# Two-layer decode attention on one core: V becomes the moving operand of the value product, in column tiles

## The chip, the cores and the metric

One core of a Trainium2 chip runs the whole program. The metric is device time in microseconds (us) of one execution, as the median of several runs. A core has five engines with an instruction queue each: TensorE (PE in the profile; PEld is its weight load), VectorE (DVE), ScalarE (ACT), GpSimd (POOL) and SyncE (SP), which here issues every transfer. Sixteen DMA engines move data between HBM and the on-chip memory SBUF. TensorE writes into PSUM, eight banks of 128 partitions by 512 fp32.

## The reference, cut to what matters

Eight sequences decode one token each through attention, a small dense block, and the same two again with the same weights and caches. The caches are 8 x 8 x 8192 x 128 in bf16, K and V, 134 MB each, and both layers need all of both.

```python
q = (x @ wq) -> 8 sequences, 32 heads, 128
k = repeat(k_cache, 4 times over heads)       # 8 cache heads, 4 query heads share one
scores = q . k * 128 ** -0.5                   # 8192 keys per sequence and cache head
p = softmax(scores)
o = p . v
x = x + o @ wo                                 # on layernorm(x)
x = x + silu(layernorm(x) @ w1) @ w2
# both steps once more
```

## The kernel before, in words

A task is (layer, sequence, cache head): 2 x 8 x 8 = 128 of them. The 8192 keys of a task are cut into four granules of 2048. A granule of K or V is one transfer of 512 KB into one of 27 slots of a large SBUF buffer (`ARENA`), 4 KB on each partition. Positions are half granules, so a task has `GPT` = 8 positions, and the main loop runs over positions `p`. The order of all work is the order of emission in that loop; each engine executes its own instructions in that order, and every wait follows from which buffers an instruction reads and writes.

The last 20 of the 32 K granules of a sequence (cache heads 3 to 7) stay in their slots from layer 0 to layer 1; these are the "kept" keys. So 352 K transfers and 512 V transfers are made, not 512 and 512. `make_tasks` orders the tasks so that, for each sequence in turn, come its five kept tasks of layer 0, then other tasks of layer 0 and 1 that load both K and V, then its five tasks of layer 1 whose keys are already there. While the kept keys of a sequence are resident, 20 of the 27 slots are taken and 7 are left for streaming; when they are used up, more slots are free. `plan_loads` gives every transfer a slot, ordered by the position that needs it; SP issues them in that order (`issue`), and waits before each until the slot's last reader, a matmul, is done.

What a task does, by position within it (`ph` = p mod 8):

- DVE transposes each loaded K granule in place, 32 x 32 words at a time (`emit_t`, L444), two positions ahead of its use.
- `emit_q` (L463, L466): four matmuls place the task's four query vectors in QSp, and DVE writes them, masked, into the stationary tile QB.
- `emit_s` (L481): at each odd position 16 matmuls score one granule. Scores are made in four column tiles of 32: tile `t` has its own 32 rows of the PSUM bank SCp.
- `softmax_max` at ph 0 of the next task (L491, L493): DVE takes the row maxima and spreads them; `softmax_shift` at ph 2 (L501 to L507): an fp32 matmul of ones sums these over partitions into OTp, and DVE picks each row's shared maximum. The exponentials are made by ACT right behind (L511).
- `softmax_sum` at ph 4 (L518, L521): row sums by DVE, joined over partitions by GpSimd's partition_all_reduce.
- `emit_pt` at ph 5 (L530, L534): TensorE transposes P, DVE copies it to PT.
- `emit_pv` (L554), `LP` = 14 positions behind the scores: 16 matmuls for each granule, each with a 128 x 128 block of V as the stationary operand and 4 probability columns, repeated `PVN` = 12 times to 48, as the moving one. The sum of a whole task stands in one bank OTp.
- `emit_norm` (L568), one position after the last of these: DVE divides by the row sums into the attention output.

When the last task of layer 0 of a sequence is normalized, a chain of small stages follows, a few per position: output projection (L652), layernorm (L576 to L612), both dense products and the query of layer 1 (L634). It has to be done before the sequence's first layer-1 task.

Of the kernel before, what the change touches and what calls it, by code (L numbers as in the profile page):

```python
# [5 lines left out]
HQ = 32  # L6
DH = 128
SM_SCALE = DH ** -0.5
# [22 lines left out]
PVN = 12  # L31
# [97 lines left out]
class Load:  # L129


    __slots__ = ("kind", "b", "g", "k", "need", "free", "slot", "after")

    def __init__(self, kind, b, g, k, need, free):
        self.kind, self.b, self.g, self.k = kind, b, g, k
        self.need, self.free = need, free
        self.slot, self.after = None, None
# [33 lines left out]
def plan_loads(tasks, kept, nslot, ngran):  # L171
# [3 lines left out]
    for i, (layer, b, g) in enumerate(tasks):  # L175
        for k in range(ngran):
            i0 = i * GPT + k * GPG
            if layer == 0 or (g, k) not in kept:
                need = -1 if i0 < PRE else i0 - LT
                last = i if layer or (g, k) not in kept else at[(1, b, g)]  # L180
                loads.append(Load("K", b, g, k, need, last * GPT + (k + 1) * GPG - 1))
# [3 lines left out]
    for d in loads:  # L185
# [3 lines left out]
        free.append((d.free, d.slot))  # L189
    return loads  # L190
# [18 lines left out]
def _build(ctx, nc, A_x, A_k_cache, A_v_cache, A_wq, A_wo, B_w1, B_w2, out):  # L209
# [64 lines left out]
    pick = sb([128, NPART, 128], BF16, "pick")  # L274
# [15 lines left out]
    PT = [sb([128, CPB, NQ * USED], BF16, "PT") for _ in range(NPT)]  # L290
    ones = sb([128, 128], FP32, "ones")
    hm = sb([128, REP], FP32, "hm")
    real = sb([128, 1], FP32, "real")
    far = sb([128, NQ * USED], FP32, "far")
    rowmax = sb([128, 1], FP32, "rowmax")
    spread = sb([128, NQ * USED], FP32, "spread")
    own = sb([128, NQ * USED], FP32, "own")
# [56 lines left out]
    k_slot = {}  # L354
    v_slot = {}

    def issue(d):
# [7 lines left out]
        (k_slot if d.kind == "K" else v_slot)[(d.b, d.g, d.k)] = d.slot  # L365

    with nc.Block() as block:

        @block.sync
        def _(sync_eng):  # L370
# [11 lines left out]
            op(dve, lambda: dve.memset(ones[:, :], 1.0), writes=["ones"])  # L382
            for n in range(NQB):
# [5 lines left out]
                    hm[:, :], lanes.rearrange("p c (r k) -> p r c k", k=NGRAN), AX.XY, ALU.add),  # L389
                reads=["ident"], writes=["hm"],  # L390
            )
            op(dve, lambda: dve.tensor_reduce(real[:, :], hm[:, :], AX.X, ALU.add), reads=["hm"], writes=["real"])
# [3 lines left out]
            for i in range(NPART):  # L396
                op(dve, lambda i=i: dve.tensor_copy(
                    pick[:, i, :].rearrange("p (a r) -> p a r", a=NQ),
                    ident[:, i // 2 * 2 * QUAD:(i // 2 + 1) * 2 * QUAD].rearrange("p (r e) -> p e r", e=2)[:, i % 2]
                    .unsqueeze(1).to_broadcast([128, NQ, QUAD])),  # L400
                   reads=["ident"], writes=["pick"])
            for c in range(NQ):
                op(dve, lambda c=c: dve.tensor_scalar(
                    far[:, c * USED:(c + 1) * USED].rearrange("p (r k) -> p r k", k=NGRAN),
# [365 lines left out]
            for p in range(NG + LP + GPT + 1):  # L770
# [8 lines left out]
                if p % GPG == GPG - 1:  # L779
                    if p < NG:  # L780
                        emit_s(p)
# [77 lines left out]
```

## Time and profile before

| | us |
|---|---|
| median of 3 runs | 1194.06 (1191.72 to 1194.8) |
| the profiled execution | 1198.79 |
| its span, first to last instruction | 1197.1 |
| DMA queue of SP, share of 16 engines' span | 99.1% |
| PE busy, VectorE busy, ScalarE busy, GpSimd busy | 839.0, 736.1, 183.5, 70.8 |
| instructions | 46189 |
| mean granted TensorE clock | 0.663 |

465.05 MB are read from HBM at 388 GB/s over the span. A busy share is an average over stages that differ: the DMA engines are busy nearly throughout, and what they move in 20 us varies between 333 and 410 GB/s. So the rate in each stage is to be read, not the share alone.

### The profile page before, as it was taken

What the parts mean: (1) busy time and instruction counts of PE and PEld (TensorE: products, weight loads), DVE (VectorE), ACT (ScalarE), POOL (GpSimd) and SP (SyncE); (2) the same over time, 40 slices, a digit from 0 to 9 for tenths busy, and PEclk for the clock granted to TensorE, in tenths of its full rate; (3) what the DMA queues carried; (4) which work ended last, traced back from release to release, by engine and by line L of the source; (5) the groups of instructions that cost most, each with busy time, mean ns of one, the idle gap of its engine ahead of it and who ended that gap; (6) DMA issues with size and microseconds to landing.
All of it is one profiled execution on the core that took longest, in us unless ns stands there. A gap on an engine that the chain in (4) does not pass through costs nothing.

```text
span 1197.1 us, 46189 instructions
## 1 busy us (share of the span) xinstructions
PE 839.0 (70%) x20984; PEld 673.4 (56%) x20984; DVE 736.1 (61%) x1830; ACT 183.5 (15%) x266; POOL 70.8 (6%) x172
## 2 busy tenths in 40 slices
PE   1636677767776677767777778777776777677785
PEld 1435566556655566556665566556665656555564
DVE  3736763767456673867457763867376755768464
ACT  0101112111111012111111111111111111111111
POOL 0000000000000000000000000000000000000000
PEclk9955568555765577655866586756775587657765
DMA  9999999999999999999999999999999999999994
GB/s 368 385 396 397 399 355 408 407 394 395 393 408 407 368 389 401 408 404 395 389 408 408 388 397 409 407 402 395 393 407 403 399 393 408 407 392 386 402 408 165
DMA packets 131619, 468.06 MB, mean 391 GB/s; under 512 B 13904, under 2 KB 19808, under 8 KB 130912
## 3 DMA queue, kind: packets, MB, share of 16 engines
q1 hardware_dynamic: 131424, 465.12, 99.1%
q8 instruction: 164, 2.69, 0.9%
q14 instruction: 31, 0.25, 0.1%
HBM read 465.05 MB, written 0.01 MB: 388 GB/s over the span
## 4 chain that ended last, share of the span: by engine, by line
DMA 40%; PE 31%; DVE 15%; issue 9%; SPq 3%; ACT 2%; POOL 0%; POOLq 0%; ACTq 0%; DVEq 0%
DMA arena<-in_A_v_cache_dram 37%; PE OTp L554 14%; PE SCp L481 8%; DVE arena L444 7%; SPq L339 3%; DMA arena<-in_A_k_cache_dram 3%; PE MISC L634 3%; PE OTp L501 2%; PE TPp L530 2%; ACT P L511 2%; DVE rowmax L491 1%; DVE PT L534 1%; PE MISC L652 1%; DVE tr L607 1%; DVE spread L493 1%
## 5 line engine op out<-in xcount | busy, mean ns | idle before, releaser
L554 PE MATMUL OTp<-PT,arena 128*128 128x48 bf16 x8192 | 381.1, 205 | 227.6 <-DMA arena<-in_A_v_cache_dram 182.1
L444 DVE STREAM_TRANSPOSE arena<-arena 128x1024 int32<-128x1024 int32 x352 | 434.9, 1236 | 115.9 <-DMA arena<-in_A_k_cache_dram 115.2
L554 PEld LDWEIGHTS OTp<-PT,arena 128*128 128x128 bf16 x8192 | 316.9, 110 | 331.5 <-DMA arena<-in_A_v_cache_dram 242.6
L511 ACT ACTIVATE P<-SCp,shift 128x512 bf16<-128x512 f32 x128 | 180.3, 1409 | 930.6 <-DVE shift L507 651.5
L481 PE MATMUL SCp<-arena,QB 128*32 128x128 bf16 x8192 | 287.0, 275 | 37.3 <-issue 29.0
L481 PEld LDWEIGHTS SCp<-arena,QB 128*32 128x32 bf16 x8192 | 161.4, 115 | 84.1 <-issue 48.6
L521 POOL PARTITION_ALL_REDUCE ssa<-ssm x128 | 55.6, 435 | 996.0 <-DVE ssm L518 970.8
L534 DVE COPY PT<-TPp 128x256 bf16<-128x256 bf16 x128 | 37.3, 291 | 103.6 <-PE TPp L530 101.8
L501 PE MATMUL OTp<-spread,ones 128*128 128x64 f32 x256 | 75.4, 389 | 25.9 <-DVE spread L493 22.7
L491 DVE TENSOR_REDUCE rowmax<-SCp 128x1 f32<-128x512 f32 x128 | 84.8, 663 | 11.5 <-PE SCp L481 10.3
L530 PE MATMUL TPp<-ident,P 128*128 128x128 bf16 x512 | 68.8, 278 | 13.7 <-ACT P L511 9.6
L504 DVE SCALAR_TENSOR_TENSOR own<-OTp,real,far 128x64 f32<-128x64 f32 x128 | 32.9, 257 | 71.7 <-PE OTp L501 71.7
L501 PEld LDWEIGHTS OTp<-spread,ones 128*128 128x128 f32 x256 | 54.9, 266 | 35.6 <-DVE spread L493 34.4
L518 DVE TENSOR_SCALAR ssm<-hm,rs 128x4 f32<-128x4 f32 x128 | 26.8, 210 | 73.9 <-ACT P L511 73.9
L530 PEld LDWEIGHTS TPp<-ident,P 128*128 128x128 bf16 x512 | 41.7, 122 | 16.5 <-ACT P L511 12.3
L634 PE MATMUL MISC<-xnT,wq 128*128 128x32 bf16 (+1 forms) x1152 | 37.1, 185 | 19.3 <-DVE xnT L621 13.1
L634 PEld LDWEIGHTS MISC<-xnT,wq 128*128 128x128 bf16 x1152 | 35.8, 105 | 20.4 <-issue 16.3
L652 PE MATMUL MISC<-at,wo 128*128 128x32 bf16 x1024 | 37.7, 185 | 6.1 <-issue 4.4
L652 PEld LDWEIGHTS MISC<-at,wo 128*128 128x128 bf16 x1024 | 33.2, 103 | 6.9 <-issue 4.6
L463 PE MATMUL QSp<-QT,pick 128*128 128x4 bf16 x512 | 32.5, 168 | 5.7 <-DVE QT L717 2.9
L493 DVE TENSOR_SCALAR spread<-ident,rowmax 128x64 f32<-128x64 bf16 x128 | 32.6, 255 | 4.5
L511 ACT ACTIVATION_READ_ACCUMULATOR P<-SCp,shift 128x1 f32 x128 | 33.3, 260 | 0.0
(54 smaller groups left out, 276.3 us busy)
## 6 DMA issues: line engine op xcount, KB each, us to landing
arena<-in_A_v_cache_dram SPq DMA_DIRECT2D x512, 512.0 KB, 10.3
arena<-in_A_k_cache_dram SPq DMA_DIRECT2D x352, 512.0 KB, 14.5
wq<-in_A_wq_dram SPq DMA_DIRECT2D x1, 4096.0 KB, 16.6
wo<-in_A_wo_dram SPq DMA_DIRECT2D x1, 4096.0 KB, 26.3
w<-in_B_w_dram SPq DMA_DIRECT2D x2, 1792.0 KB, 22.8
P<-in_A_x_dram SPq DMA_DIRECT2D x1, 8.0 KB
out_dram<-P SPq DMA_DIRECT2D x1, 8.0 KB
```

The lines of the kernel that those rows point to most:

```text
L444: op(dve, lambda: dve.transpose(words, words), reads=[r_half(slot, 0), r_half(slot, 1)], writes=[r_half(slot, 0), r_half(slot, 1)])
L481: lambda n=n, t=t: pe.matmul(SCp[bank][t * QUAD:(t + 1) * QUAD, k * 128:(k + 1) * 128], QB[qn][:, n, :], keys[:, t, n // 2, n % 2], start= ...
L491: op(dve, lambda: dve.tensor_reduce(rowmax[:, :], SCp[bank][:, :], AX.X, ALU.max), reads=[f"SC{bank}"], writes=["rowmax"])
L493: op(dve, lambda: dve.tensor_scalar(spread[:, :].rearrange("p (c q) -> p c q", q=USED), lanes, rowmax[:, 0:1], -SM_SCALE, op0=ALU.mult, op ...
L501: mm_group([lambda: pe.matmul(every, ones[:, :], spread[:, :], start=True, stop=True)], reads=["ones", "spread"], writes=[f"OT{ob}"])
L511: op(act, lambda: act.activation(P[:, :].rearrange("p (x j k) -> p k x j", x=CPB, k=NGRAN), SCp[bank][:, :].rearrange("p (k x j) -> p k x ...
L521: op(pool, lambda: pool.partition_all_reduce(ssa[st][:, :], ssm[st][:, :], 128, bass.bass_isa.ReduceOp.add), reads=[f"ssm{st}"], writes=[f ...
L530: lambda c=c: pe.transpose(tpv[:, c, :], P[:, c * 128:(c + 1) * 128], ident[:, :])
L534: op(dve, lambda: dve.tensor_copy(PT[pb][:, :, :].rearrange("p x (c q) -> p x c q", q=USED), tpv.rearrange("p x (c q) -> p x c q", q=QUAD) ...
L554: lambda c=c, cc=cc: pe.matmul(otp, chunk(slot, h * GRP + c), pv[:, cc % CPB, cc // CPB % NQ, k, :].unsqueeze(2).to_broadcast([128, REP, P ...
L634: lambda o=o, k=k: pe.matmul(MISC[:, o * n:o * n + w], w_sb[:, k, o * 128:(o + 1) * 128], rhs_of(k).to_broadcast([128, w]) if n == 1 else ...
L652: lambda o=o, h=h: pe.matmul(MISC[:, o * w:(o + 1) * w], wo_sb[:, h, o * 128:(o + 1) * 128], rhs_of(h).to_broadcast([128, w]) if n == 1 el ...
```

## The change

The value product is turned round. V is now the moving operand, 512 columns at a time, and 16 probability columns of one column tile (4 blocks `x` of keys times 4 query rows) are the stationary one. Four matmuls, one for each column tile `t`, do a granule. Each tile has 16 rows of the OTp bank, and of the 512 output columns of a row only the 128 of its own block `x` are wanted. Two ways pick them out. In most tasks ACT copies the whole bank to SBUF as fp32 (`emit_own`, tile E), and four accumulated fp32 matmuls against a selection matrix `sel` (`emit_fold`) join the 64 rows and four blocks into the 128 x 4 result. In the 40 tasks with kept keys in layer 1 (`eased`), four DVE operations add up the own blocks by masks and one fp32 matmul joins them. The result lands in the first columns of OTp as before, and the normalization reads it three positions later than before (`FOLD`).

Two more changes: kept keys of layer 1 are scored two slots at a time, 256 moving columns in each of 16 matmuls, where the distance of the two slots fits (`REACH`), and kept slots come free by pairs; to keep that distance positive the contents of the two slots of a pair may be exchanged, so a transposed slot is looked up by `turn`. And the row maxima are joined over partitions by GpSimd's partition_all_reduce in place of the matmul of ones, with smaller DVE operations around it. The query matmuls now make all heads of a sequence at once (16 matmuls for 8 tasks), and the copy to PT goes from DVE to ACT. The number and size of K and V transfers are unchanged.

```diff
@@ plan_loads
-                loads.append(Load("K", b, g, k, need, last * GPT + (k + 1) * GPG - 1))
+                loads.append(Load("K", b, g, k, need, (last * GPT + (k // PAIR + 1) * PAIR * GPG - 1
+                                  if last != i or PAIR_ALL else last * GPT + (k + 1) * GPG - 1)))
...
+    for pair in keys.values():
+        ks = sorted(d.k for d in pair)
+        for d, k in zip(sorted(pair, key=lambda d: d.slot), ks):
+            d.k = k
@@ emit_q
-                for i in range(NPART):
-                    at = (n * NPART + i) * REP
-                    steps.append(lambda i=i, at=at: pe.matmul(
-                        QSp[:, at:at + REP], pick[:, i, :], q, start=True, stop=True))
+                if ti == span_of[(layer, b)][0]:
+                    emit_queries(layer, b)
...
@@ emit_s
+                two = PAIR_ALL or not has_t(i)
+                if two and k % PAIR != PAIR - 1:
+                    return
+                slots = [k_slot[(b, g, k - n)] for n in range(PAIR - 1, -1, -1)] if two else [t_slot[(b, g, k)]]
+                step = (slots[-1] - slots[0]) * SLOT
...
+                if two and step <= REACH:
+                    runs = [(k - PAIR + 1, k + 1, both)]
...
@@ softmax_max
-                op(dve, lambda: dve.tensor_scalar(
-                    spread[:, :].rearrange("p (c q) -> p c q", q=USED), lanes, rowmax[:, 0:1], -SM_SCALE,
-                    op0=ALU.mult, op1=ALU.mult),
-                   reads=["ident", "rowmax"], writes=["spread"])
+                op(dve, lambda: dve.scalar_tensor_tensor(
+                    top[:, :], hm[:, :], rowmax[:, 0:1], far[:, :], op0=ALU.mult, op1=ALU.add),
+                   reads=["hm", "rowmax", "far"], writes=["top"])
+                op(pool, lambda: pool.partition_all_reduce(tops[:, :], top[:, :], 128, bass.bass_isa.ReduceOp.max),
+                   reads=["top"], writes=["tops"])
@@ softmax_shift
-                mm_group([lambda: pe.matmul(every, ones[:, :], spread[:, :], start=True, stop=True)],
-                         reads=["ones", "spread"], writes=[f"OT{ob}"])
-
                 op(dve, lambda: dve.scalar_tensor_tensor(
-                    own[:, :], every, real[:, 0:1], far[:, :], op0=ALU.mult, op1=ALU.add),
-                   reads=[f"OT{ob}", "real", "far"], writes=["own"])
-                op(dve, lambda: dve.tensor_reduce(shift[:, :], own[:, :], AX.X, ALU.min), reads=["own"], writes=["shift"])
+                    mine[:, :], tops[:, :], -SM_SCALE, hm[:, :], op0=ALU.mult, op1=ALU.mult),
+                   reads=["tops", "hm"], writes=["mine"])
+                op(dve, lambda: dve.tensor_reduce(shift[:, :], mine[:, :], AX.X, ALU.add), reads=["mine"], writes=["shift"])
@@ emit_pt
-                op(dve, lambda: dve.tensor_copy(
-                    PT[pb][:, :, :].rearrange("p x (c q) -> p x c q", q=USED),
-                    tpv.rearrange("p x (c q) -> p x c q", q=QUAD)[:, :, :, 0:USED]),
+                op(act, lambda: act.copy(
+                    PT[pb][:, :, :, :, :].rearrange("p a t x r -> p x t a r"),
+                    tpv.rearrange("p x (t q) -> p x t q", q=QUAD)[:, :, :, 0:USED].rearrange("p x t (a r) -> p x t a r", r=REP)),
                    reads=[f"TP{tb}"], writes=[f"PT{pb}"])
@@ emit_pv
-                        lambda c=c, cc=cc: pe.matmul(
-                            otp, chunk(slot, h * GRP + c), pv[:, cc % CPB, cc // CPB % NQ, k, :].unsqueeze(2).to_broadcast([128, REP, PVN]),
-                            start=(cc == 0), stop=(cc == NCH - 1),
-                        )
+                steps = [
+                    lambda t=t: pe.matmul(
+                        OTp[ob][t * QUAD:t * QUAD + CPB * REP, :], PT[pb][:, k, t].rearrange("p x r -> p (x r)"),
+                        ARENA[:, slot * SLOT + t * KB:slot * SLOT + (t + 1) * KB],
+                        start=(k == 0), stop=(k == NGRAN - 1),
+                    )
+                    for t in range(NQ)
+                ]
+            def emit_own(ti):
+                ob = ti % 2
+                if not eased(ti) and ACT_FOLD:
+                    op(act, lambda: act.copy(E[:, :], OTp[ob][:, :]), reads=[f"OT{ob}"], writes=["E"])
+                    return
+                for x in range(CPB):
...
+                        op(dve, lambda x=x, ot=ot: dve.scalar_tensor_tensor(
+                            E[:, 0:DH], ot, own_x[:, x:x + 1], E[:, 0:DH], op0=ALU.mult, op1=ALU.add),
+                           reads=[f"OT{ob}", "own_x", "E"], writes=["E"])
+            def emit_fold(ti):
...
+                        lambda x=x: pe.matmul(OTp[ob][:, 0:REP], E[:, x * DH:(x + 1) * DH], sel[:, x, :],
+                                              start=(x == 0), stop=(x == CPB - 1))
+                        for x in range(CPB)
...
+                    steps = [lambda: pe.matmul(OTp[ob][:, 0:REP], E[:, 0:DH], hm[:, :], start=True, stop=True)]
@@ main loop
+                copied = p - LP - GPT
+                if copied >= 0 and copied % GPT == 0 and copied // GPT < ntask:
+                    emit_own(copied // GPT)
+                folded = p - LP - GPT - FOLD_AT
+                if folded >= 0 and folded % GPT == 0 and folded // GPT < ntask:
+                    emit_fold(folded // GPT)
...
-                done = p - LP - GPT
+                done = p - LP - GPT - FOLD
```

Constants: `PAIR` = 2, `REACH` = 32767, `FOLD` = 3, `FOLD_AT` = 2, `ACT_FOLD` on, `PAIR_ALL` off. In the startup, `pick`, `ones` and their fills go, and `own_x`, `sel` and two clears of OTp come.

## The prediction

> **What bounds the kernel now.** I read the page's transfer part first, then the rates by stage, then what the transfers wait for.
>
> ```profile
> DMA  9999999999999999999999999999999999999994
> GB/s 368 385 396 397 399 355 408 407 394 395 393 408 407 368 389 401 408 404 395 389 408 408 388 397 409 407 402 395 393 407 403 399 393 408 407 392 386 402 408 165
> q1 hardware_dynamic: 131424, 465.12, 99.1%
> q8 instruction: 164, 2.69, 0.9%
> DMA arena<-in_A_v_cache_dram 37%; PE OTp L554 14%; PE SCp L481 8%; DVE arena L444 7%; SPq L339 3%; DMA arena<-in_A_k_cache_dram 3%; PE MISC L634 3%; PE OTp L501 2%; PE TPp L530 2%; ACT P L511 2%; DVE rowmax L491 1%; DVE PT L534 1%; PE MISC L652 1%; DVE tr L607 1%; DVE spread L493 1%
> ```
>
> The engines are never without packets, the rate is either 407 to 409 GB/s or clearly less, and V transfers head the chain. So the change, which moves the same caches, can only win what lies between a slice's rate and 408. The second line to see is q8: the instructions themselves come through the same 16 engines, in 164 blocks of 16 KB.
>
> Four stages (columns: stage, its length, PE, PEld, DVE, ACT and POOL busy, clock, DMA share, GB/s):
>
> ```profile
> 470.00:515.00 45.00, 32.87 (x761) 25.86 (x761) 30.07 (x64) 7.05 (x10) 2.16 (x5) 0.63 1.03 407
> 390.00:410.00 20.00, 13.93 (x307) 10.81 (x305) 13.52 (x26) 2.81 (x4) 0.83 (x2) 0.50 0.97 349
> 160.00:175.00 15.00, 11.68 (x361) 10.24 (x357) 9.97 (x20) 2.83 (x4) 0.44 (x1) 0.73 0.85 305
> 300.00:320.00 20.00, 16.39 (x470) 14.17 (x471) 11.48 (x34) 2.83 (x4) 0.89 (x2) 0.73 1.01 382
> ```
>
> and what a K transfer takes to land, first in 470:515, then in 390:410:
>
> ```profile
> arena<-in_A_k_cache_dram SPq DMA_DIRECT2D x16, 512.0 KB, 15.6
> ...
> arena<-in_A_k_cache_dram SPq DMA_DIRECT2D x8, 512.0 KB, 7.5
> ```
>
> A transfer of 0.524 MB takes 1.285 us at 408 GB/s. So some 12 are in flight in the first stage and 5 or 6 in the second, where the kept keys leave 7 slots. Every long stretch with 15 us runs at 407; the losses stand where the queue is short. I take the whole span in rows of 20 us and add up (408 - rate) / 408 x 20. From 80 to 1160 us this is 26.8 us: 14.1 us in the ten rows in which a chain's dense stages and query run (160, 300, 440, 560, 580, 700, 820, 840, 960, 1100), 10.9 us in thirteen rows with a short queue, most of it right after the queue gets short (380 and 400 alone 2.9), and 1.8 us scattered. Startup and end are apart.
>
> TensorE in a plain stretch (start, length, ..., [idle before and releaser]):
>
> ```profile
> 271.27 0.82 PE L554 MATMUL OTp<-PT,arena 128*128 128x48 bf16 x16 [0.70 <-DMA arena<-in_A_v_cache_dram]
> 272.16 0.69 PE L501 MATMUL OTp<-spread,ones 128*128 128x64 f32 x2
> 272.78 0.62 PE L481 MATMUL SCp<-arena,QB 128*32 128x128 bf16 x16
> 274.28 0.82 PE L554 MATMUL OTp<-PT,arena 128*128 128x48 bf16 x16 [0.88 <-DMA arena<-in_A_v_cache_dram]
> ```
>
> A granule pair (K and V, 2.57 us) leaves TensorE 0.7 to 1.05 us of waiting for V: it frees slots in time, with little to spare.
>
> **Part by part.**
>
> *Instructions.* Per task there were 64 matmuls for PV, 64 for scores, 4 transposes, 4 query ones and 2 of L501: 138, each with a weight load. Now 88 tasks have 16 + 64 + 4 + 2 and 8 for the fold (L501 shows two instructions for one fp32 matmul): 94. The 40 eased ones have 16 + 32 + 4 + 2 + 2 = 56. That is 88 x 88 + 40 x 164 = 14,300 of 46,189 instructions gone, 31% (28% if no pair of slots fits). At 2.69 MB for all, 0.83 MB less to move: **-2.0 us** (ends -1.8 and -2.3).
>
> *Blocks and the short queue.* A 16 KB block holds up one engine of the sixteen, all others go on, and a K or V transfer has landed only when the last engine has done its share; a long queue hides that until it gets short. That this is the 10.9 us is my inference: it fits where the loss stands, and no row shows it alone. Around such a place 5 of 16 tasks are eased, so instructions there fall by 41%; of 10.9 us: **-4.5 us**. Ends 0 (another cause) and -8.
>
> *PV.* Before: 16 matmuls start to next work in 0.65 us at the half clock. After: 4 tiles of 512 columns. The nearest row is L481, which puts the same 512 columns through each of four tiles in 0.55 us, weight loads included; four serial ones would take 16 x 0.107. I take 0.55, so V's slot is free 0.1 us sooner. Hidden in plain stretches by the wait for V.
>
> *Fold.* Four fp32 matmuls with 128 x 128 weights. The nearest row is L501's pair: 0.69 us in all, of which second weight load starts 0.17 and second matmul 0.27 us after the first. Eight at 0.17 to 0.27: 1.4 to 2.2, plus 0.3 to drain; I take 1.8 at the half clock. It comes after one granule in four: 0.55 + 1.8 + 0.55 = 2.9 against 2.57 us per granule, 0.3 over, and the next granule has 0.9 to make it good. In return L501 (0.62, and 0.2 of waiting for `spread`) goes. Per plain task of 10.3 us TensorE is about even: -0.4 PV, -0.8 L501, -0.1 queries, +1.8. What queues behind the fold are the next score and PV, and behind them the slots; cost taken 0 under five queued transfers (6.4 us), upper end +14 (rival below), lower end -1.
>
> *Eased tasks.* No K to transpose, scores by pairs, one fp32 matmul in place of four: TensorE saves some 2 us of a task of 5.2. The four DVE additions (each nearest to L504's 0.257, 128 columns wide 0.32) are 1.3 us on an engine busy 7 of 20 us there. This follows directly on each chain, where TensorE is at 16.4 of 20 us: the queue refills sooner. Also the page has 74.5 and 48.6 us of weight loads idle for "issue", in stalls up to 2.9 us, of which a third should go. I take a fifth of the 14.1 us: **-3.0 us**. Ends -8, and +5, because `FOLD` starts the chain three positions later with its end fixed: some 22 stages in 18 positions, not 21. Then layernorm's last stage and the first product stand one position apart, not three, and TensorE waits for xnT, about 1 us in each of 7 chains.
>
> *Maxima by GpSimd.* DVE gives up `spread` (0.255) and the long `own` (0.257) for two of 4 columns (L518's row: 0.21), and its 71.7 us of waiting for L501. The reduce is in the trace: L521 0.435 us, and 0.1 from DVE and back. Between `top` and `mine` stands a transposition (1.24 us): hidden. Without that cover, in eased tasks, 0.6 us on a DVE with nothing queued. 0; ends -1, +2.
>
> *Copies on ACT.* PT is 256 elements, E 512; L682's two rows (14 elements 184 ns, 112 elements 265) give 0.83 ns each, L511 2.8 (its store is strided). So PT 0.4 to 0.9 and E 0.6 to 1.6 us, on an engine idle 85%. PT is wanted two positions later, after a score of 0.55 and a V wait of 0.75: covered. 0; ends -1, +2.
>
> *End.* After the last V nothing hides anything: PV -0.2, E +0.6, fold +1.9, two handoffs +0.1: **+2.4 us** (ends +1.6, +3.9). *Start:* 0; SP's long issue of the weights sets it.
>
> Sum: -2.0 - 4.5 - 3.0 + 2.4 = **-7.1 us**. The profiled execution, 1198.79, stands 4.7 over the median of the runs (1194.06) and would come to 1191.7; a median of like runs to **1187.0**.
>
> Two rules of the Trainium skill I weighed. The stages above move 407 GB/s. "DMA: Bandwidth & Descriptors", Specifications, gives HBM about 358 GB/s per core; by it 468.06 MB need 1307 us and nothing could be won. The trace disagrees, and the measurement decides. ACT here loads its tables once (1283 ns). "ScalarE: Activation LUTs", Table sets, says that cheap functions such as copy are in every set, so no reload; no run here shows a copy yet.
>
> **The rivals.**
>
> *Nothing reaches the end* (transfers bound it anyway): the short-queue losses have another cause. -2.0 + 2.4, and up to 3 either way: 1191 to 1197. For it: 99.1%. Against: the rates differ by stage.
>
> *The fold's burst decides* (slower). If its eight passes do not overlap, it takes 8 x (0.27 + 0.2) = 3.8 us. The burst is then 0.55 + 3.8 + 0.55 = 4.9 us, 2.3 over a granule, of which the next makes good some 0.5. The price: in 300:320 the query's four parts of 1.05 us cost 26 / 408 x 20 = 1.3 us, 0.3 for each us. With 47 plain tasks at a short queue (some 480 us of 10.3), each us not made good costs 47 x 0.3 = 14: here 25, and with the -7.1 of the forecast +18, 1212. It decides from half a us not made good, a fold of about 2.5 us. For it: L501's two matmuls take 0.69. Against: nearly half of that is the drain.
>
> *More than that*: all 23 rows at 404: -22 - 2 + 2.4, 1172.
>
> *Others* (column tiles one after the other, 2 us a granule; table reloads of 2 x 1.28 us a task): 1220 and more. Against: L481's 0.55.
>
> **How the numbers follow.** Forecast case 0.47, 1180 to 1191; more 0.10, 1170 to 1180; nothing 0.20, 1191 to 1198; fold 0.16, 1198 to 1220; others 0.07. The likeliest is 1187.0. The range 1177 to 1205 leaves out the lower part of "more", the upper of "fold", and "others". A measurement of this kernel tells 0.3%, 3.6 us, from no change: faster 0.57, same 0.20, slower 0.23.
>
> **What would show it.** Right: q8 near 115 blocks; rows after the queue gets short at 380 or more, deep ones still at 407; the fold's eight matmuls under 2.2 us; the last V's landing to the end about 2.4 us longer (15 before). Wrong: PE or PEld waiting for E or PT, SP waiting longer for the fold's followers, rates under 380 once in each plain task, or a clock that falls and makes PV 0.8 us.

## The result, and the profile after

The changed kernel takes 1201.1 us (median of 7 runs, 1200.1 to 1206.4) against 1194.8 us (7 runs) of the kernel before on the same chip: a ratio of 1.0055, 95% interval 1.0032 to 1.0079, some 6.5 us slower. The forecast was 7 us faster. The profiled execution took 1203.2 us with a span of 1201.2.

From the page of the changed kernel, the rates by slice, the two instruction queues and the chain that ended last:

```profile
GB/s 363 385 396 407 399 376 409 408 403 379 396 409 408 392 357 410 408 399 383 400 409 403 393 391 409 409 392 365 403 408 397 365 396 409 408 404 385 385 409 133
q8 instruction: 109, 1.79, 0.6%
q14 instruction: 35, 0.29, 0.1%
DMA arena<-in_A_v_cache_dram 48%; SPq L356 15%; DMA arena<-in_A_k_cache_dram 10%; PE OTp L608 5%; PE OTp L640 3%; PE MISC L721 3%; DVE arena L466 3%; PE SCp L543 3%; ACT P L570 1%; PE TPp L589 1%; DVE E L632 1%; DVE tr L694 1%; DVE yr L696 1%; DVE rowmax L554 0%; PE MISC L739 0%
```

The deep slices still run at 407 to 410. But there are new holes (357, 365, 365) where the kernel before had 389, 395 and 399. V transfers head the chain with 48% in place of 37%, and SP's issue of loads (L356) has 15% of it in place of 3%: more of the time hangs on transfers and on when they were issued.

From the same page the groups that the change brought (line, engine, operation, count | busy us, mean ns | idle time before, and what ended most of it):

```profile
L608 PE MATMUL OTp<-arena,PT 128*16 128x512 bf16 x2048 | 283.0, 549 | 292.8 <-DMA arena<-in_A_v_cache_dram 289.9
L640 PE MATMUL OTp<-sel,E 128*128 128x4 f32 x704 | 147.9, 333 | 0.9 <-ACT E L624 0.7
L559 POOL PARTITION_ALL_REDUCE tops<-top x128 | 47.5, 371 | 563.1 <-DVE QT L655 241.6
L593 ACT COPY PT<-TPp 128x256 bf16<-128x256 bf16 x128 | 47.6, 372 | 211.7 <-PE TPp L589 211.7
L624 ACT COPY E<-OTp 128x512 f32<-128x512 f32 x88 | 52.1, 592 | 4.1 <-PE OTp L608 4.1
```

PV is 0.55 us a granule; the two ACT copies are 0.37 and 0.59 us. The fold is the one new thing that weighs: 148 us of TensorE in the 88 plain tasks (those that are not eased), 1.68 us each on average and 1.87 us in one piece at the half clock.

Rows of 20 us before (length, busy times of PE, PEld, DVE, ACT and POOL, clock, DMA share, GB/s), a place where the queue gets short and three where a chain runs:

```profile
400.00:420.00 20.00, 13.51 (x296) 10.39 (x292) 13.30 (x32) 1.95 (x3) 1.23 (x3) 0.50 0.99 371
420.00:440.00 20.00, 14.67 (x439) 12.88 (x442) 17.87 (x51) 2.55 (x6) 1.66 (x4) 0.76 1.02 407
680.00:700.00 20.00, 14.11 (x392) 11.85 (x393) 17.49 (x56) 3.00 (x5) 2.45 (x6) 0.75 1.03 407
940.00:960.00 20.00, 15.61 (x408) 13.14 (x404) 16.68 (x49) 2.99 (x5) 2.46 (x6) 0.60 1.02 401
```

The same rows of the changed kernel:

```profile
400.00:420.00 20.00, 12.71 (x223) 7.76 (x224) 14.02 (x38) 4.53 (x8) 2.41 (x6) 0.50 1.01 403
420.00:440.00 20.00, 16.38 (x391) 12.86 (x387) 14.10 (x41) 3.88 (x7) 1.97 (x5) 0.64 0.99 359
680.00:700.00 20.00, 14.77 (x304) 10.81 (x296) 16.52 (x51) 4.28 (x9) 2.68 (x7) 0.59 0.99 376
940.00:960.00 20.00, 13.49 (x292) 9.63 (x292) 15.38 (x44) 3.99 (x8) 2.38 (x6) 0.67 0.97 362
```

Where the queue gets short the change won in three places what the prediction hoped for (371 to 403, and likewise 377 to 394 at 260, 381 to 400 at 660); in three others it lost 8 to 11 GB/s (at 520, 780 and 920). One row later, where the chain starts, it lost more (407 to 359). Summed as in the prediction from 80 to 1160 us, the rows lost 26.8 us before and 30.8 after. The prediction's ten rows with a chain are not where the loss is: they lose 13.1 us in place of 14.1. It stands in rows beside them, where the chains now begin: 280, 420, 680, 800 and 940 lose 9.5 us together in place of 0.9.

What happens there, in TensorE's timeline after, from 416 to 432 (start, length, [idle before and what ended it]):

```profile
416.43 0.61 PE L608 MATMUL OTp<-arena,PT 128*16 128x512 bf16 x4 [1.53 <-DMA arena<-in_A_v_cache_dram]
...
419.05 1.72 PE L721 MATMUL MISC<-xnT,w 128*128 128x32 bf16 x56 [1.47 <-DVE xnT L699]
420.70 0.62 PE L543 MATMUL SCp<-arena,QB 128*32 128x128 bf16 x16
421.11 0.64 PE L608 MATMUL OTp<-arena,PT 128*16 128x512 bf16 x4
421.67 1.87 PE L640 MATMUL OTp<-sel,E 128*128 128x4 f32 x8
...
424.45 1.73 PE L721 MATMUL MISC<-hsT,w 128*128 128x32 bf16 x56
...
431.58 0.61 PE L608 MATMUL OTp<-arena,PT 128*16 128x512 bf16 x4 [3.06 <-DMA arena<-in_A_v_cache_dram]
```

TensorE stands 1.47 us for the LayerNorm's output, and the next granule's matmuls stand behind it in its queue. Then come the first dense product (w1), the fp32 fold and the second product (w2) within 8 us, without a gap to make the delay good. K and V slots come free late, and their loads are issued late. SP's timeline there:

```profile
417.12 0.33 SPq L356 DMA_DIRECT2D arena<-in_A_v_cache_dram  x1
421.41 0.33 SPq L356 DMA_DIRECT2D arena<-in_A_k_cache_dram  x1
421.84 0.38 SPq L356 DMA_DIRECT2D arena<-in_A_v_cache_dram  x1
```

For 4 us no load is issued; the next two go out right after the score and V matmuls that stood behind w1. The loads issued in this stretch take up to 9.5 us to land, and 9.7 us after the V load of 421.84 TensorE comes out of a wait of 3.06 us for V. In the kernel before, w1 waits for nothing at this place, and V is waited for 0.45 to 1.41 us at a time:

```profile
421.99 1.74 PE L634 MATMUL MISC<-xnT,w 128*128 128x32 bf16 x56
...
433.69 0.76 PE L554 MATMUL OTp<-PT,arena 128*128 128x48 bf16 x16 [1.41 <-DMA arena<-in_A_v_cache_dram]
```

The end, from the last copy on (same columns):

```profile
1184.45 0.58 ACT L624 COPY E<-OTp 128x512 f32<-128x512 f32 x1 [4.14 <-PE OTp L608]
1185.09 1.87 PE L640 MATMUL OTp<-sel,E 128*128 128x4 f32 x8 [0.69 <-ACT E L624]
1186.99 0.16 DVE L655 TENSOR_TENSOR QT<-OTp,rcp 128x4 bf16<-128x4 f32 x1 [4.42 <-PE OTp L640]
```

From the last V's landing to the end it is 18.5 us against 15.1: 3.3 more. In the kernel before, the normalization follows the last V matmul directly:

```profile
1182.00 0.82 PE L554 MATMUL OTp<-PT,arena 128*128 128x48 bf16 x16 [0.29 <-DMA arena<-in_A_v_cache_dram]
1182.86 0.16 DVE L568 TENSOR_TENSOR QT<-OTp,rcp 128x4 bf16<-128x4 f32 x1 [3.65 <-PE OTp L554]
```

### The profile page after: what moved, and what is told of

It reads as the page before. It is cut to its first block, busy times and chain, and to the rows that moved or that the text cites. A ratio compares the mean times of both kernels' runs of the same rounds, so it can differ in the third digit from the quotient of the medians.

```text
span 1201.2 us, 32533 instructions
## 1 busy us (share of the span) xinstructions
PE 811.5 (68%) x13960; PEld 505.4 (42%) x13960; DVE 735.7 (61%) x1858; ACT 274.0 (23%) x482; POOL 117.9 (10%) x300
## 4 chain that ended last, share of the span: by engine, by line
DMA 59%; PE 15%; SPq 15%; DVE 7%; issue 3%; ACT 1%; POOL 1%; POOLq 0%; ACTq 0%; DVEq 0%
DMA arena<-in_A_v_cache_dram 48%; SPq L356 15%; DMA arena<-in_A_k_cache_dram 10%; PE OTp L608 5%; PE OTp L640 3%; PE MISC L721 3%; DVE arena L466 3%; PE SCp L543 3%; ACT P L570 1%; PE TPp L589 1%; DVE E L632 1%; DVE tr L694 1%; DVE yr L696 1%; DVE rowmax L554 0%; PE MISC L739 0%
## 5 line engine op out<-in xcount | busy, mean ns | idle before, releaser
L608 PE MATMUL OTp<-arena,PT 128*16 128x512 bf16 x2048 | 283.0, 549 | 292.8 <-DMA arena<-in_A_v_cache_dram 289.9
L543 PE MATMUL SCp<-arena,QB 128*32 128x128 bf16 (+1 forms) x7040 | 275.6, 301 | 3.7 <-DVE mine L563 2.3
L608 PEld LDWEIGHTS OTp<-arena,PT 128*16 128x16 bf16 x2048 | 54.9, 97 | 383.6 <-DMA arena<-in_A_v_cache_dram 375.6
L640 PEld LDWEIGHTS OTp<-sel,E 128*128 128x128 f32 x704 | 140.3, 296 | 37.8 <-issue 25.6
L640 PE MATMUL OTp<-sel,E 128*128 128x4 f32 x704 | 147.9, 333 | 0.9 <-ACT E L624 0.7
L559 POOL PARTITION_ALL_REDUCE tops<-top x128 | 47.5, 371 | 563.1 <-DVE QT L655 241.6
L593 ACT COPY PT<-TPp 128x256 bf16<-128x256 bf16 x128 | 47.6, 372 | 211.7 <-PE TPp L589 211.7
L624 ACT COPY E<-OTp 128x512 f32<-128x512 f32 x88 | 52.1, 592 | 4.1 <-PE OTp L608 4.1
L632 DVE SCALAR_TENSOR_TENSOR E<-OTp,own_x,E 128x128 f32<-128x128 f32 x120 | 42.1, 351 | 4.3
L645 PE MATMUL OTp<-hm,E 128*128 128x4 f32 x80 | 20.5, 327 | 24.1 <-DVE E L632 24.1
```

Of the source, the lines that this page charges most:

```text
L543: lambda n=n, t=t, lo=lo, hi=hi, of=of: pe.matmul(SCp[bank][t * QUAD:(t + 1) * QUAD, lo * 128:hi * 128], QB[qn][:, n, :], of(t, n), start= ...
L608: lambda t=t: pe.matmul(OTp[ob][t * QUAD:t * QUAD + CPB * REP, :], PT[pb][:, k, t].rearrange("p x r -> p (x r)"), ARENA[:, slot * SLOT + t ...
L632: op(dve, lambda x=x, ot=ot: dve.scalar_tensor_tensor(E[:, 0:DH], ot, own_x[:, x:x + 1], E[:, 0:DH], op0=ALU.mult, op1=ALU.add), reads=[f" ...
L640: lambda x=x: pe.matmul(OTp[ob][:, 0:REP], E[:, x * DH:(x + 1) * DH], sel[:, x, :], start=(x == 0), stop=(x == CPB - 1))
```

## The experiments

Two theories to begin with: **late**, that the loss comes from the normalization and the chain that starts behind it coming three positions later (`FOLD` 3), and **burst**, that it comes from the fp32 fold. Ratios are to the kernel before on the same chip; 0.01 is 12 us.

### Three positions later, on the kernel before

Normalization and the bookkeeping behind it, three positions later (the loop runs three positions longer too; cut):

```
-                done = p - LP - GPT
+                done = p - LP - GPT - 3
```

> The kernel before with one thing of the change alone: the normalization, and with it the start of each sequence's chain, 3 positions later. Theory 'chain' (the later start squeezes the chain's stages against its fixed end, TensorE waits for the normalized input and the products come bunched): 3 to 4 us slower than before, 1198, with new losses in the rows 280, 420, 680, 940 and 1100 where the changed kernel has them. Theory 'fold' (the 1.87 us burst of eight fp32 passes holds up scores, PV and so the slots): within 1 us of before.

1.0140 [1.0125, 1.0154], some 17 us where either theory gave 4 at most. In the trace TensorE waits 18.1 us in 23 pieces for the late normalization before L501, which writes the same bank. So that wait is mixed in. The next leaves the normalization alone and moves the bookkeeping only (heads ready for the output projection, start of the chain):

```
                     emit_norm(done // GPT)
+                late = done - 3
+                if late >= 0 and late % GPT == 0 and late // GPT < ntask:
+                    tj = late // GPT
```

> The kernel before, its normalization where it was, and only the bookkeeping behind it (the head given to the output projection, the start of the chain) 3 positions later. In the run with the normalization itself 3 positions later, TensorE's matmul of ones also waited 18.1 us for the normalization, on the bank that the two share. Theory 'chain': most of that run's 16 us stays without this wait, ratio 1.007 to 1.012. Rival 'bank': the shared bank made it, ratio 1.002 to 1.004.

1.0114 [1.0096, 1.0133], some 13.6 us, on a kernel with no fold at all. *Late* holds without the bank. The prediction had put this at 5 us at most.

### Normalization early, and picks in bfloat16

Early, on the changed kernel:

```
-FOLD = 3
-FOLD_AT = 2
+FOLD = 1
+FOLD_AT = 1
```

> The changed kernel with the fold at one position after the copy and the normalization right behind it (2 positions earlier than in the change, 1 later than in the kernel before); the burst itself stays. Theory 'chain': most of the loss goes, 1197 to 1198. Theory 'fold': no change, 1200 to 1202.

1.0082 [1.0062, 1.0103]: not faster. Picks in bfloat16 (in plain tasks `E` and `sel` are rounded to bfloat16; eased tasks keep an fp32 `E32`):

```
-    E = sb([128, CPB * DH], FP32, "E")
+    E = sb([128, CPB * DH], BF16, "E")
+    selb = sb([128, CPB, REP], BF16, "selb")
...
-lambda x=x: pe.matmul(OTp[ob][:, 0:REP], E[:, x * DH:(x + 1) * DH], sel[:, x, :],
+lambda x=x: pe.matmul(OTp[ob][:, 0:REP], E[:, x * DH:(x + 1) * DH], selb[:, x, :],
```

> The changed kernel with the bank copied to SBUF as bf16 and picked by bf16 products in the plain tasks (E is rounded to bf16 there, which the change does not do); the times of all stages stay. The fold should fall from 1.87 to about 0.6 us. Theory 'fold': 4 us or more faster than the changed kernel, under 1197, of which 1.3 us at the end of the program. Theory 'chain': only the 1.3 us at the end, 1200.

0.9995 [0.9982, 1.0009]. Both together:

> Both of the last two edits. If both theories hold a part, this is the fastest of the three, 1190 to 1194, at or under the kernel before; if only 'chain' holds, as the early one less 1.3 us, 1196; if only 'fold' holds, as the bf16 one.

**0.9897 [0.9884, 0.9911]**, 1183.8 us: faster than both kernels, and called the best version below. The fold is 0.27 us here in place of 1.87. So the change holds a gain of some 12 us, and the fp32 fold and the late start together eat 19. They don't add up: the fold alone (early) costs 22, the late start alone (bfloat16) 12. The waits of the early fp32 version show why (waiting, for whom: us, times, longest):

```profile
DVE at L655 <- PE OTp L640: 151.2, 62, 3.9
PE TPp L589 <- ACT P L570: 74.9, 74, 2.4
```

With bfloat16 picks, just as early:

```profile
DVE at L658 <- PE OTp L643: 56.2, 61, 1.8
```

The transposes wait for the exponentials twice as long as in the best version (37.8 us). An early normalization makes VectorE stand 2.4 us at a time, 62 times, behind the fp32 fold, with the next task's softmax in its queue. Three positions later that wait is 13.4 us in all, and the chain pays in its stead. As far as these runs go, `FOLD` chooses only who pays.

With bfloat16 picks and the normalization two positions behind the copy (`FOLD` 2):

> The kernel with bf16 picks and the fold one position after the copy, the normalization 2 positions after the copy (1 in the early one, 3 in the change): a dose in between. Theory 'chain': between 0.9897 and 0.9995, about 0.994. Rival (VectorE's wait for the fold, 56 us in the early one, costs as much as the chain gains): at or under 0.988.

0.9938 [0.9917, 0.9959]: with 0.9897 at one position and 0.9995 at three, 5 to 7 us a position.

### Which part of late: the normalization or the chain

From the best version; the normalization stays early, the bookkeeping comes two positions later (as in `b_chain3`, with `CHAIN` 2):

> The version with bfloat16 picks and the normalization one position after the copy (ratio 0.9897), in which only the bookkeeping behind the normalization (the list of heads ready for the output projection, and the start of the chain between the layers) waits two positions more; the normalization stays. 'Chain' (what the change lost by normalizing late is the late start of the chain, which has a fixed end) expects the whole loss of the version with bfloat16 picks and the normalization three positions behind: a ratio of 0.9975 to 1.001, 9 to 13 us, and the rows at the chains below 400 GB/s. 'Bank' (the late normalization itself holds up the bank of the output, so the matmuls behind it) expects 0.988 to 0.992, nothing lost. Between them each has a share.

1.0007 [0.9990, 1.0024]. The whole loss of late is there; it is the chain's (with the attention heads handed to the output projection, which the edit delays too).

### How a late chain costs

Written out by position from the code, in six of the eight chains all stages from w1 on stand at the same positions however late the chain starts, because its end is fixed (the first and the last chain move as a whole). What a late start does is to put two stages on one position at the chain's beginning. Two ideas: it is the doubling (*squeeze*), or it is the room lost between the LayerNorm's last stage and the first matmul on its output. First, the late chain without its empty stages:

```
-SETTLE = 2
+SETTLE = 0
```

> The version whose chain between the layers starts two positions later (ratio 1.0007) without the chain's four empty stages (two behind each LayerNorm, SETTLE 0 in place of 2): fewer stages in as many positions, so that hardly any position gets two. 'Squeeze' (late start costs because the stages come two to a position against a fixed end) expects most of the 13 us back: a ratio of 0.990 to 0.995. 'Room behind the norm' (the empty stages hide the time to xnT, and matmuls that come without them hold TensorE up for it) expects 1.0007 or worse, up to 1.01, with more waits of TensorE for xnT.

1.0043 [1.0031, 1.0056]: worse than late itself, though nothing is doubled any more. *Squeeze* does not explain the loss: what both have is one position between a LayerNorm and its matmul, here at both LayerNorms. Nor does the late chain double more work than the early one: both put the same two pairs of working stages on one position, and what the late start adds are pairs with an empty stage. TensorE's waits without the empty stages:

```profile
PE MISC L725 <- DVE xnT L703: 12.2, 7, 1.8
PE MISC L725 <- DVE QT L659: 19.0, 7, 2.9
```

The first is w1 behind the first LayerNorm; the second is the query behind the second one (in the trace at 436 us, VectorE makes `QT` directly behind `xnT`). The late chain with its empty stages has 11.3 us of the first and none of the second. Two positions in place of three hurt an early chain too (`SETTLE` 1, with `PAIR` 1):

> The version with ratio 0.9897 with the kept keys scored slot by slot (0.9882 by itself) and one empty stage in place of two behind each LayerNorm of the chain. 'Squeeze' expects a further gain, 0.984 to 0.9875; 'room behind the norm' a loss, 0.989 to 0.993.

1.0026 [1.0013, 1.0040], where `PAIR` 1 alone has 0.9882: 17 us lost. TensorE waits 15 times for the chain's LayerNorm there, 26.8 us, against 4 times and 1.1 us.

Now the room given back without starting earlier: the two dense projections whole, in one stage each, so that the late chain needs two positions fewer:

```
-st = block_stages(xs, ["XT0", "XT1", "XT2"], 1, True)
+st = block_stages(xs, ["XT0", "XT1", "XT2"], 1, False)
```

> The version with bfloat16 picks, early normalization and a late chain (ratio 1.0007), with the chain's two projections of the dense block each emitted whole at one position in place of halves at two. That makes the chain two stages shorter, so that it starts just as late and no stage before the first projection has to go to the position of another: three positions between the LayerNorm's end and the first matmul on its output, as in the version with an early chain; one is left there without this edit. 'Room behind the norm' expects most of the 13 us back, a ratio of 0.989 to 0.994, and TensorE waiting under 2 us in all for that LayerNorm's output (11 us without the edit). 'Late is late' (any later start costs, by vector work that collides with the softmax) expects 0.998 to 1.002.

0.9935 [0.9916, 0.9955]: 8.6 of the 13 us come back, with the start as late as before. Waits with the late chain and its halves (waiting, for whom: us, times, longest):

```profile
PE MISC L725 <- DVE xnT L703: 11.3, 9, 1.6
DVE eh L778 <- ACT eh L773: 9.3, 9, 2.0
```

and with whole projections:

```profile
PE MISC L725 <- DVE hsT L780: 7.4, 8, 1.9
PE MISC L725 <- DVE xnT L703: 2.2, 6, 0.5
DVE eh L778 <- ACT eh L773: 2.0, 1, 2.0
```

Most of the wait for `xnT` goes, and so does most of VectorE's wait for the SiLU's exponential. A new one of 7.4 us for `hsT` comes; that it is the 4.5 us still missing was not tried. From the LayerNorm's last stage to w1 it is three positions in the kernel before, in the best version and here, two at `FOLD` 2 and one in the change, in the six chains named above. One rival stays: an early chain with whole projections was not run, so a part of the 8.6 us could come from the whole projections themselves and not from the room.

The same edit on the change itself, fp32 fold and `FOLD` 3 kept:

> The change itself with the same one edit: the two projections of the dense block whole at one position each. The fp32 picks and their burst of 1.87 us stay, and the normalization stays three positions behind the copy. 'Room behind the norm' expects a ratio of 0.994 to 0.999 in place of 1.0055, that is, the change faster than or level with the kernel before; 'late is late' 1.003 to 1.008.

1.0001 [0.9987, 1.0014] in place of 1.0055: some 6.5 us back by one word. TensorE's wait for the chain's `xnT` is 1.0 us in place of 7.7, and the prediction's ten rows with a chain lose 4.7 us in place of 13.1. The same rival holds here.

### Is it the length of the burst

The best version with the four bfloat16 matmuls of the fold repeated; each repetition begins its sum anew, so that the same four columns come out (the expectation below says otherwise):

```
-                        for x in range(CPB)
+                        for _n in range(TIMES) for x in range(CPB)
```

> The same version (ratio 0.9897) with the four bfloat16 matmuls that fold a plain task's output issued four times over into the same four columns (each start clears the sum... the first, ninth and so on are overwritten, the output's value is not kept): the output's sum is not what the reference wants, and that is all that changes. At the 0.3 to 0.4 us that the four take in bfloat16 this makes a burst of 1.3 to 1.7 us, near the 1.87 us of the fp32 burst of the change, but with the copy of the output in bfloat16 and the normalization early. 'Burst' (the fp32 fold costs by its length on TensorE alone: the score and V matmuls behind it start late, and DVE waits for it) expects most of the 1.85 points between this version and the same with fp32 picks: a ratio of 1.002 to 1.008. 'Other' (the cost of fp32 picks is their weight loads, their clock or the copy in fp32, not the length of the burst) expects 0.989 to 0.995.

0.9905 [0.9892, 0.9918]. But the sixteen matmuls take 0.59 us, not 1.3 to 1.7: some 27 ns for each more. So 0.3 us of burst costs 1 us by the medians, and a long one had still to be run, 15 times over:

> The version with bfloat16 picks and early normalization (ratio 0.9897), the four matmuls of the fold issued 15 times over (each repetition begins its sum anew, so the same four columns come out). Sixteen took 0.59 us in the run with four repetitions, 28 ns for each more, so 60 take about 1.85 us, as long as the fp32 fold of the change. 'Length' (a burst on TensorE costs by its length, in front of score matmuls and of the normalization) expects the ratio of the version with fp32 picks and early normalization, 1.004 to 1.010. 'Something else of fp32' (the copy in fp32, weight loads) expects 0.991 to 0.998.

1.0238 [1.0219, 1.0257], more than either theory gave. The burst is 1.76 us, which is also the mean of the early fp32 version. Beside that version (1.0082), first its groups:

```profile
L640 PEld LDWEIGHTS OTp<-sel,E 128*128 128x128 f32 x704 | 147.0, 309 | 40.8 <-issue 22.6
L640 PE MATMUL OTp<-sel,E 128*128 128x4 f32 x704 | 154.7, 343 | 0.8 <-ACT E L624 0.7
```

and of the 15-fold one, with its instruction queue and VectorE's wait:

```profile
L644 PEld LDWEIGHTS OTp<-selb,E 128*128 128x128 bf16 x5280 | 146.9, 103 | 47.9 <-issue 29.3
L644 PE MATMUL OTp<-selb,E 128*128 128x4 bf16 x5280 | 154.6, 166 | 7.0 <-issue 6.2
q8 instruction: 145, 2.38, 0.8%
DVE at L659 <- PE OTp L644: 148.1, 62, 3.3
```

Two bursts with the same busy time, the same time in weight loads and nearly the same wait of VectorE (151.2 and 148.1 us): so that wait comes from the burst's length, whatever the type. The two versions differ in 9,153 instructions (41,683 and 32,530), 36 blocks in q8 (145 and 109), and in TensorE's matmuls idle for "issue", that is, with nothing to wait for that the profile shows: 23.2 against 2.9 us. And in time, by 18.7 us.

The kept traces, taken packet by packet, tell what "issue" is here. In the 15-fold version TensorE stops 19 times for more than 0.3 us between two matmuls of one line, and all 19 stops end 1.0 to 1.8 us after a block of q8 has landed; in the kernel before it is 43 of 43. By chance it would be about one in ten. So TensorE stood for its instructions. What a block costs isn't linear, and the idle time is no price: 8 or 9 blocks more cost nothing in `eb_single` and some 1 us in `eb_burst4`, and `b_pool` below idles 13 us more for "issue" than the kernel before (92.0 and 78.9) and is no slower.

### Blocks of instructions

To price the blocks alone, waits that are already fulfilled were added to the best version: 110 on GpSimd after each join of the row sums; then on ScalarE, 100 behind the exponentials of each task and 100 behind each copy of a plain task's output; then on GpSimd, 72 after each of its two joins. The first, cut to the added lines:

```
+                for _ in range(BLANK):
+                    pool.wait_ge(syn.eng_sem[dve.engine], 1)
```

> The early kernel with bf16 picks and 110 waits that are already fulfilled on GpSimd's queue in each task, behind the join of the row sums: some 14,000 instructions more, as many as the change took away, about 1.9 us of an idle engine per task. Theory 'blocks' of the prediction (16 KB instruction blocks hold up one of the sixteen engines, and the short queue pays): blocks back to about 160, 6 us slower, ratio 0.995. Rival: the blocks cost their bytes alone, 2 us, 0.991.

1.0229 [1.0209, 1.0248].

> The same version (ratio 0.9897) with waits already fulfilled added to ScalarE where it is idle: 100 behind the exponentials of each task and 100 behind each copy of a plain task's output, some 10,800 more instructions, and as many blocks of instructions to fetch as the change took away (some 90 of 8 KB in the second queue of instructions). ScalarE has 3.4 us and 4.5 us to the next work at these places, and 50 instructions take about 2.1 us, so that its own work isn't late. 'Blocks' (each block holds up one of the 16 DMA engines, and that is what the short queue loses; the prediction took 4.5 us for some 50 blocks of twice the size) expects 3 to 8 us more, a ratio of 0.992 to 0.996. 'No blocks' (they go beside the rest) expects 0.988 to 0.991.

1.0515 [1.0501, 1.0529].

> The version with ratio 0.9897 with waits already fulfilled on GpSimd: 72 behind each join of the maxima and 72 behind each join of the row sums, which the build packs two to an instruction, some 9,200 instructions and 70 to 80 more blocks of 8 KB. At 42 ns they take 1.5 us, where GpSimd stands idle for 3 us and more behind both joins, so the joins aren't late. 'Blocks' expects 2 to 5 us more, a ratio of 0.9915 to 0.994; 'no blocks' 0.989 to 0.991. If vector work waits for the joins longer than before (12 us in all by then), the run says nothing on it.

1.0297 [1.0278, 1.0316]. None of the three tells: q8 stays at 107, all new blocks are in q14 (91, 119 and 107 in place of 35), and the added work makes its own engine late. On GpSimd such an instruction lasts 42 ns, but in the trace the next one starts 87 ns after it, so that the waits took at least twice the time that the expectations give them. From the third:

```profile
DVE mine L569 <- POOL tops L563: 54.4, 41, 2.1
```

against 20.4 us in 41 pieces of at most 0.5 without the waits. On ScalarE the copy of `PT` starts some 2.5 us after its transposes start, and not at once: without the waits it could start 0.7 us after the exponentials, since the transposes follow them directly, and the waits stand in between. What the runs do show is that neither GpSimd, idle nine tenths of the time, nor ScalarE has time to give at these places: the joins and `PT` are on the way to the next V matmul. Whether a block costs transfer rate by itself stays open.

### Maxima and pairs by themselves

The kernel before with the maxima joined on GpSimd, nothing else:

> The kernel before with the row maxima joined on GpSimd and nothing else of the change. The prediction put it at 0, with ends -1 and +2. Theory 'relief' (the matmul of ones, 0.62 us and its waits, and VectorE's 71.7 us of waiting for it go): 2 to 4 us faster, 0.997. Rival 'latency': within 0.1% of before, or slower.

0.9988 [0.9975, 1.0000]: 1.4 us, and 3 at most. The best version with kept keys scored slot by slot:

```
-PAIR = 2
+PAIR = 1
```

> The same version (ratio 0.9897) with the kept keys scored slot by slot (PAIR = 1): 2304 score matmuls over 128 columns in place of 1152 over 256. 'Fewer instructions' (pairs save the issue of matmuls and free TensorE in the layer that is short of it) expects a ratio of 0.991 to 0.996, 2 to 7 us lost in rows of the second layer. 'Nothing there' (the second layer's tasks with kept keys wait for V, not for TensorE; and a pair is scored one position later than its first slot alone) expects 0.987 to 0.991, no loss or a small gain.

0.9882 [0.9869, 0.9895], no slower than with pairs: the pairs bring nothing here. By its median, 1183.2 us, it is the fastest of all kernels run, though its interval overlaps that of the best version.

## Why the prediction was wrong

Two steps failed, the chain and the fold. By the prices below, either alone would have left the sum at zero or a little faster; both together made the change slower.

- **Eased tasks and chain, -3.0 with an upper end of +5: the first step that failed.** It names the mechanism word for word (LayerNorm's last stage and the first product one position apart, TensorE waiting for `xnT`), and it sized the direct wait about right: 7.7 us in 5 pieces, where it had said 1 us in each of 7 chains (by position it is six). Wrong was to book the wait one to one, and as an end of the range and not as a term. Giving the room back is worth 6.5 us on the change itself (`a_whole`); the late start costs 13 to 14 us where nothing else holds the chain up (`eb_chain2`, `b_chain3`). A wait of TensorE in front of queued score and V matmuls delays the slots, and so the loads: behind 1.47 us at 419 there were 4 us without an issue, and then 3.06 us without V at 431.6. With 6.5 for this and 7 for the fold, the sum of -7.1 comes to +6.4; measured is +6.5. That this fits so well is luck in part: 2.6 of the 7 are at the end, for which the sum already has 2.4; the two prices don't add up in the runs; and the terms on blocks and eased tasks were not measured by themselves.
- **Fold, cost 0: the second step that failed.** Its length was right: 1.87 us against 1.8 with ends 1.4 and 2.2. That five queued transfers cover it was not: bfloat16 picks gain 7 us with a late normalization and 22 with an early one. Of the 7 us, 2.6 are at the end (18.5 us from the last V's landing in the change, 15.9 in `a_bf16`). The rival *the fold's burst decides* named the right burst, with a point too high: it was to decide from 2.5 us of length, and at 1.87 it already costs. The path is another than it gave, at least in the early versions: there VectorE waits behind the burst, with the softmax in its queue. By which path the other 4 to 5 us are lost in the change itself was not traced.
- **Instructions, -2.0.** 13,656 fewer instructions (14,300 foreseen), q8 at 109 blocks (115), 0.90 MB (0.83). The sizes are right; the price was not measured by itself.
- **Blocks and the short queue, -4.5.** Some of the rows right after the queue gets short rose as foreseen, others fell. The cause that I inferred, a block that holds up one DMA engine, was not shown. What was seen is that TensorE itself stood for its instructions: "issue" took 78.9 us of its matmuls' time in 62 pieces before, 2.3 us in 4 after. For the two rows of weight loads that the prediction named it went from 123.1 to 45.4 us, more than the third expected, but other weight loads took most of that up (162.1 us in all before, 151.7 after); what went there are the long stalls. By the two bursts above, 20 us of it can go with 18.7 us of time; by `b_pool`, 13 us more of it can cost nothing. So the term stays unproven. "Runtime: NRT & Kernel Launch" of the Trainium skill, Instruction fetch mechanics, calls the fetching of instructions in blocks of 16 KiB mostly hidden. The pieces of up to 2.8 us in the trace before disagree.
- **PV**, 0.55: measured 0.549. **Copies on ACT**, 0: 0.37 us (0.4 to 0.9 foreseen) and 0.59 us (0.6 to 1.6), waited for little. The profile of the changed kernel lists 216 copies and still one table load (1283 ns). That agrees with "ScalarE: Activation LUTs" of the Trainium skill, Table sets, by which copy is in every set. **Maxima**, 0 with -1 and +2: -1.4. **End**, +2.4 with ends 1.6 and 3.9: +3.3.
- Two side sums of the prediction are off, and neither enters the -7.1: without pairs the instructions fall by 25% (88 x 88 + 40 x 100 of 46,189), not 28%, and 23 rows at 404 win 20.5 us, not 22.
- *Nothing reaches the end* is wrong: the fastest version is 14 us faster than the kernel before. *More than that* (22 us less by its sum, 1172) was not reached; the fastest version gets two thirds of that.
- The granted clock fell from 0.663 to 0.600, as the prediction feared, and that does not explain the loss: the fastest kernel runs at 0.591.

## What to carry to other kernels

When a new step lengthens the road from one engine's result to another's use, count the positions left between producer and first consumer on every road behind it, not only on its own, and book the wait with all that stands behind it in the queue. An engine that is idle nine tenths of the time can still be on the path, and a fixed end with stages pulled together eats the room at the beginning first. Look there before trading precision or moving the step: here two projections emitted whole, in one stage each, gave 6.5 us back.

## What the hardware showed that I had not expected

- Small matmuls overlap far more in bfloat16 than in fp32: 60 of 128 x 128 by 4 columns took 1.76 us, some 27 ns from one start to the next; four fp32 ones, eight instructions, took 1.87 us.
- TensorE can stand for its own instructions in the middle of a group of matmuls, for up to 2.6 us: all 43 such stops of more than 0.3 us in the kernel before end 1.0 to 1.8 us after a block of q8 has landed. Of two kernels with bursts equal in busy time, the one with 9,153 instructions more is 18.7 us slower; a difference of nine blocks (107 and 116) isn't felt.
- Waits already fulfilled are cheap only singly: in bulk on GpSimd one such instruction started every 87 ns, and 53 in a row took 4.6 us.
- A join over the partitions of 128 x 4 on GpSimd takes 0.37 us for a maximum and 0.43 for a sum.
